# First layer of a two-block stack: the order of LayerNorm work on VectorE, and how the last output tile is cut

## Chip, cores, metric

The kernel runs on one core of one Trainium2 chip. The metric is the device time of one execution in microseconds (us). Before the change the median of four executions is 1633.42 us (1633.33 to 1634.01).

A core has five engines with a queue of instructions each: TensorE (PE: matrix products; its weight loads are listed apart as PEld), VectorE (DVE), ScalarE (ACT), GpSimd (POOL) and SyncE (SP, which here issues all DMA transfers). An engine takes its instructions in order. An instruction that has to wait holds up all that stand behind it on the same engine.

## What is computed

The input is x, 2048 tokens by 1024 features in bf16. Two blocks alternate, A, B, A, B, each with a LayerNorm ahead of it and a residual sum behind it:

```python
def _A_ref(x, wqkv, wo):           # linear attention, 32 heads of 32
    ...
    q, k, v = qkv[0], qkv[1], qkv[2]
    phi = lambda t: jnp.where(t > 0, t + 1, jnp.exp(t)) + 1e-6
    pq, pk = phi(q), phi(k)
    kv = jnp.einsum("bhsd,bhse->bhde", pk, v)
    z = jnp.einsum("bhsd->bhd", pk)
    num = jnp.einsum("bhqd,bhde->bhqe", pq, kv)
    den = jnp.einsum("bhqd,bhd->bhq", pq, z)[..., None] + 1e-6
    o = num / den
    return (...o...) @ wo

def _B_ref(x, w_gate, w_up, w_down):
    g = jnp.einsum("bsd,df->bsf", x, w_gate)
    u = jnp.einsum("bsd,df->bsf", x, w_up)
    h = g * u
    return jnp.einsum("bsf,fd->bsd", h, w_down)

x = x + _A_ref(_layernorm(x, axis=-1), A_wqkv, A_wo)
x = x + _B_ref(_layernorm(x, axis=-1), B_w_gate, B_w_up, B_w_down)
...
```

The last two lines run twice; the inner width of block B is 3584.

## The kernel before

The tokens are cut into 16 tiles of 128 (`NT`), four tiles to a group (`TPG`). `X` holds all of them on the core, and is the residual stream. The instructions of each engine stand in the order in which the program text emits them; no scheduler moves them. So "ahead of" in the text is "ahead of" in the queue.

**A unit of the first layer.** `k_unit(t)` and `q_unit(t)` are 16 matmuls each: 8 slices of the feature axis, times two halves of 512 output columns (`both`, line 204). The stationary operand is `xT`, the normalised tile t turned so that features lie on the partitions. `phi` (lines 209 to 214) follows: ScalarE makes `e` = exp and the positive part from the PSUM tile, then VectorE makes min(e, 1) + eps (line 213) and adds the two (line 214). The PSUM tiles that units use (`mm`) rotate through three buffers, and ScalarE is their last reader. `e` rotates through three buffers too, freed by line 214.

**What a unit needs.** `norm(t)` makes `xT` for tiles 4 to 15, in three steps. `ln_stats(t)`: VectorE takes two half-row statistics (line 183) and joins them to mean and variance (line 185), then GpSimd adds epsilon (line 187) and takes the power -1/2 (line 189), which gives `rstd`. `ln_apply(t)`: VectorE writes the normalised tile into `XN` (line 194) and needs `rstd` for it. `turn` (line 198): SP issues a transposing DMA from `XN` into `xT`. Tiles 0 to 3 are handled apart at the very start: they are only centred, turned by TensorE, and their `rstd` goes in as the scale inside `phi`. So their `XN` must be normalised later by a separate `ln_apply`, and only the products behind the q and k units (`g_unit`) read it.

**The order around the change.** After tiles 0 to 3 have had their k units, VectorE gets four `ln_apply` for tiles 0 to 3. Then `weave(main, fill)` alternates one entry of each list. `main` is q0 to q3, k4 to k7, q4 to q7, k8 to k15. `fill` is `norm(4)` to `norm(15)`, then `zs(...)` entries. Each `zs` adds the k rows of one or more tiles onto the running sum `zacc` (line 258). After the weave come `zs(13, 14, 15)` and `z_split` (lines 262, 263), which splits `zacc` into two bf16 parts. TensorE goes on with `g_unit(0)`, `g_unit(1)` and then `z_sum`, whose matmuls read these two parts.

**The end.** The last tile of the last layer is computed in pieces by `d_end` (line 487 for the matmuls), each piece 28 matmuls over the inner width, followed by a residual sum on VectorE (line 468) and a store to the output (line 470). All other tiles go through `d_unit` in one piece of 1024 columns.

Of the kernel before, what the change touches and what calls it, by code (L numbers as in the profile page):

```python
# [15 lines left out]
def weave(main, fill, first=0, step=1):  # L16

    out, fill = [], list(fill)
    for i, u in enumerate(main):
        out.append(u)  # L20
        if fill and i >= first and (i - first) % step == 0:
            out.append(fill.pop(0))
    return out + fill
# [3 lines left out]
def kernel(  # L27
# [15 lines left out]
    NT = S // P  # L43
# [4 lines left out]
    TPG = G // P  # L48
# [27 lines left out]
    def rows(ap, n):  # L76
        return ap.rearrange("p (t n) -> p t n", n=n)
# [85 lines left out]
    def mm_tile():  # L163
        return psum.tile([P, 2, NB], F32, tag="mm", bufs=3, name="ps")
# [7 lines left out]
    def idle(n):  # L172
        for _ in range(n):
            nc.tensor.matmul(out=zps[:, 0, :], lhsT=xT[3][:, 0, 0:P], rhs=xT[3][:, 0, :], start=True, stop=True)
# [5 lines left out]
    def ln_stats(t):  # L180
        st = small.tile([P, 2, 6], F32, tag="st", name="st")
        for c in range(2):
            nc.vector.bn_stats(out=st[:, c, :], in_=X[:, t, c * NB:(c + 1) * NB])  # L183
        mv = small.tile([P, 2], F32, tag="mv", bufs=NT, name="mv")
        nc.vector.bn_aggr(out=mv[:], in_=st[:])  # L185
        ve = small.tile([P, 1], F32, tag="ve", name="ve")
        nc.gpsimd.tensor_scalar(out=ve[:], in0=mv[:, 1:2], scalar1=1e-5, scalar2=None, op0=ALU.add)  # L187
        rstd = small.tile([P, 1], F32, tag="rstd", bufs=NT, name="rstd")
        nc.gpsimd.tensor_tensor(out=rstd[:], in0=ve[:], in1=mhalf[:], op=ALU.pow)  # L189
        stat[t] = (mv, rstd)  # L190

    def ln_apply(t, dst):
        mv, rstd = stat[t]
        nc.vector.tensor_scalar(out=dst, in0=X[:, t, :], scalar1=mv[:, 0:1], scalar2=rstd[:],  # L194
                                op0=ALU.subtract, op1=ALU.mult)

    def turn(src, slot, tl):
        nc.sync.dma_start_transpose(out=xT[slot][:, :, tl * P:(tl + 1) * P], in_=src)
# [22 lines left out]
    def layer_A(li):  # L221
        first = li == 0
        XN, PK = (rows(R1[:], D), rows(R2[:], D)) if first else (rows(R2[:], D), rows(R1[:], D))
# [6 lines left out]
        def k_part(t, a, b):  # L230
            if a == 0:
                open_ps[t] = mm_tile()
            ps = open_ps[t]
            tl = t % TPG
            for k in range(a, b):
                both(ps, xT[t // TPG][:, k, tl * P:(tl + 1) * P], wkv[:, k, :], k == 0, k == KD - 1)
            if b == KD:
                phi(ps, PK[:, t, :], scale_of(t))

        def k_unit(t):  # L240
            return lambda: k_part(t, 0, KD)
# [4 lines left out]
        def q_unit(t, later=None):  # L246
            def run():
                ps = mm_tile()
                tl = t % TPG
                for k in range(KD):  # L250
                    both(ps, xT[t // TPG][:, k, tl * P:(tl + 1) * P], wq[:, k, :], k == 0, k == KD - 1)
                phi(ps, q_slot(t), scale_of(t), later)
            return run

        def z_unit(t):
            def run():
                in0 = PK[:, 0, :] if t == 1 else zacc
                nc.vector.tensor_tensor(out=zacc, in0=in0, in1=PK[:, t, :], op=ALU.add)
            return run
# [77 lines left out]
        def norm(t, stats=True):  # L337
            def run():
                if stats:
                    ln_stats(t)  # L340
                ln_apply(t, XN[:, t, :])
                turn(XN[:, t, :], t // TPG, t % TPG)
            return run

        def zs(*ts):
            return lambda: [z_unit(t)() for t in ts]

        if first:
            def centre(t, mean):
                nc.vector.tensor_scalar(out=XN[:, t, :], in0=X[:, t, :], scalar1=mean, scalar2=None, op0=ALU.subtract)  # L350

            pts = {}

            def turn_pe(t):
                if t == 1:
                    pts[t] = psum.tile([P, KD, P], BF16, tag="mm", bufs=3, name="pt1")
                else:
                    pts[t] = psum.tile([P, KD, P], BF16, tag="kv", bufs=1, name="pt")
                for k in range(KD):
                    nc.tensor.transpose(out=pts[t][:, k, :], in_=XN[:, t, k * P:(k + 1) * P], identity=ident[:])  # L360
                nc.scalar.copy(out=xT[0][:, 0:4, t * P:(t + 1) * P], in_=pts[t][:, 0:4, :])

            def turn_rest(t):
                nc.vector.tensor_copy(out=xT[0][:, 4:8, t * P:(t + 1) * P], in_=pts[t][:, 4:8, :])

            mean1 = small.tile([P, 1], F32, tag="mean1", bufs=1, name="mean1")
            junk = small.tile([P, D], BF16, tag="eb", bufs=3, name="junk")

            idle(9)
            ln_stats(0)  # L370
            centre(0, stat[0][0][:, 0:1])
            nc.scalar.activation(out=junk[:], in_=X[:, 1, :], func=ACT.Copy, scale=1.0 / D, accum_out=mean1[:])  # L372
            turn_pe(0)
            idle(1)
            centre(1, mean1[:])
            turn_pe(1)
            ln_stats(2)
            centre(2, stat[2][0][:, 0:1])
            turn_rest(0)
            turn_rest(1)  # L380
            for t in range(2):
                k_part(t, 0, 2)
            for t in range(2):
                k_part(t, 2, 3)
            turn_pe(2)
            for t in range(2):
                k_part(t, 3, 4)
            ln_stats(3)
            centre(3, stat[3][0][:, 0:1])
            turn_rest(2)  # L390
            ln_stats(1)
            k_part(2, 0, 4)
            turn_pe(3)
            turn_rest(3)
            for t in range(3):
                k_part(t, 4, 8)
            k_part(3, 0, 8)
            for t in range(TPG):
                ln_apply(t, XN[:, t, :])
            main = [q_unit(t) for t in range(4)] + [k_unit(t) for t in range(4, 8)] + [q_unit(t) for t in range(4, 8)]  # L400
            main += [k_unit(t) for t in range(8, 16)]
            fill = [norm(t) for t in range(4, 16)]
            fill += [zs(1, 2), zs(3, 4), zs(5, 6), zs(7), zs(8), zs(9), zs(10, 11), zs(12)]
            do(weave(main, fill))
            do([zs(13, 14, 15), z_split])
        else:
            main = [k_unit(t) for t in range(4)] + [q_unit(t) for t in range(4)]
            main += [k_unit(t) for t in range(4, 8)] + [q_unit(t) for t in range(4, 8)]
            main += [k_unit(t) for t in range(8, 16)]
            fill = [norm(t, False) for t in range(12, 16)]  # L410
            fill += [zs(1), zs(2), zs(3)] + [lambda: None] * 2
            fill += [zs(4), zs(5), zs(6), zs(7)] + [lambda: None] * 3 + [zs(8), zs(9), zs(10), zs(11)]
            do(weave(main, fill))
            do([zs(12, 13, 14, 15), z_split])
# [22 lines left out]
        fill = [lambda t=t: ln_stats(t) for t in range(4)] + [b_norm(t) for t in range(4)]  # L437
# [5 lines left out]
    def b_norm(t, stats=False):  # L443
        def run():
            if stats:
                ln_stats(t)
            xn = tail[t % 2]
            ln_apply(t, xn)
            turn(xn, t // TPG % 2, t % TPG)
        return run  # L450
# [16 lines left out]
    def add_store(t, a, b, ps, last):  # L467
        nc.vector.tensor_tensor(out=X[:, t, a:b], in0=X[:, t, a:b], in1=ps, op=ALU.add)  # L468
        if last:
            nc.sync.dma_start(out=o_view[:, t, a:b], in_=X[:, t, a:b])  # L470
# [10 lines left out]
    def d_end(t):  # L481
        def run():
            tl = t % TPG
            for a, b in ((0, 512), (512, 768), (768, 1024)):
                ps = mm_tile()
                for f in range(KF):
                    nc.tensor.matmul(out=ps[:, 0, 0:b - a], lhsT=hT[:, f, tl * P:(tl + 1) * P], rhs=wd[f][:, a:b],  # L487
                                     start=(f == 0), stop=(f == KF - 1))
                add_store(t, a, b, ps[:, 0, 0:b - a], True)
        return run  # L490

    def do(units):
        for u in units:
            u()
# [37 lines left out]
    def prefetch(i, last):  # L532
# [6 lines left out]
        return run  # L539

    layer_A(0)
    layer_B(1)
    layer_A(2)
    layer_B(3)

# [29 lines left out]
```

## Time and profile before

| | us |
|---|---|
| median of four executions | 1633.42 |
| the profiled execution, its own time | 1634.01 |
| its span, first to last instruction | 1632.1 |
| TensorE busy in the span | 1618.0 |
| VectorE busy | 608.3 |
| ScalarE busy | 287.1 |
| GpSimd busy | 53.7 |

The granted TensorE clock is 1.00 over the whole span. A profile line of a group reads: start, duration, engine, source line, operation, what is written from what, shapes, count, and in brackets how long the engine had been idle just before and what ended that. A matmul's recorded duration is longer than the distance to the next one, since matmuls are pipelined: a stretch of equal matmuls is read from start to start. Times of the span count from its first instruction.

The VectorE work in the stretch that the change touches, by mean duration of one instruction (ns):

| line | what | mean ns |
|---|---|---|
| 183 | statistics of half a tile (two per tile) | 682 |
| 185 | joining them | 209 |
| 194 | normalising a tile | 543 |
| 213 | phi, first step | 424 |
| 214 | phi, sum | 693 |
| 258 | adding a tile to `zacc` | 1222 |
| 468 | residual sum, 1024 / 512 / 256 columns | 1222 / 689 / 421 |

### The profile page before, as it was taken

How to read it: one execution, taken by the hardware profiler on the slowest of the kernel's cores; microseconds unless marked ns; L12 is line 12 of the kernel's file. 1: busy time of each engine (PE TensorE's matmuls, PEld its weight loads, DVE VectorE, ACT ScalarE, POOL GpSimd, SP SyncE). 2: the span in 40 equal slices, each digit the busy share in tenths (PEclk: the TensorE clock that was granted, in tenths of full speed). 3: DMA queues.
4: the chain of work that ended last, by engine and by line, in shares of the span. 5: the costliest groups of instructions: out<-in, count | busy, mean ns of one | idle time of the engine just before them, and what ended most of it. 6: DMA issues, size and time to landing. Idle time of an engine off the chain costs nothing.

```text
span 1632.1 us, 17617 instructions
## 1 busy us (share of the span) xinstructions
PE 1618.0 (99%) x7510; PEld 743.0 (46%) x7662; DVE 608.3 (37%) x889; ACT 287.1 (18%) x386; POOL 53.7 (3%) x141
## 2 busy tenths in 40 slices
PE   9999999999999999999999999999999999999999
PEld 4444444444444444444444444444444444444444
DVE  6799853211311221243245698432123113211111
ACT  5523201100110110011045222011011101101110
POOL 1100000000000000010000000000000000000000
DMA  6324755521550453142420258565226405521400
GB/s 219 65 65 110 233 161 159 163 66 52 143 192 1 120 166 102 48 150 66 87 63 1 78 104 232 155 174 161 65 88 176 143 20 174 161 65 65 155 0 27
DMA packets 234686, 182.56 MB, mean 112 GB/s; under 512 B 100080, under 2 KB 215408, under 8 KB 234608
## 3 DMA queue, kind: packets, MB, share of 16 engines
q1 hardware_dynamic: 234608, 181.43, 38.3%
q8 instruction: 60, 0.98, 0.3%
q14 instruction: 18, 0.15, 0.0%
HBM read 153.09 MB, written 4.19 MB: 96 GB/s over the span
## 4 chain that ended last, share of the span: by engine, by line
PE 98%; DVE 1%; issue 1%; DMA 0%; POOL 0%; ACT 0%; SPq 0%; DVEq 0%
PE ps L204 49%; PE ps L460 47%; PE ps L487 1%; PE kv L301 0%; DVE st L183 0%; PE pm L204 0%; DMA X<-in_A_x_dram 0%; DMA xT<-R 0%; DVE PQ L214 0%; POOL rstd L189 0%; DVE R L194 0%; PE pt L360 0%; ACT junk L372 0%; ACT PQ L210 0%; DVE e L213 0%
## 5 line engine op out<-in xcount | busy, mean ns | idle before, releaser
L460 PE MATMUL ps<-xT,R 128*128 128x512 bf16 x2382 | 525.9, 379 | 2.7
L460 PEld LDWEIGHTS <-R 128*128 128x128 bf16 x2432 | 238.0, 98 | 286.9
L464 DVE TENSOR_TENSOR R<-gs,ps 128x512 bf16<-128x512 f32 x224 | 154.0, 688 | 533.3 <-ACT gs L463 533.3
L204 PEld LDWEIGHTS <-R 128*128 128x128 bf16 x2248 | 219.8, 98 | 264.5 <-issue 0.3
L463 ACT COPY gs<-ps 128x512 f32<-128x512 f32 x224 | 131.3, 586 | 1039.2 <-PE ps L460 1013.4
L460 PE MATMUL ps<-xT,W 128*128 128x512 bf16 x1130 | 250.1, 379 | 1.1
L204 PEld LDWEIGHTS <-xT 128*128 128x128 bf16 x1536 | 149.3, 98 | 179.2 <-DMA xT<-R 1.8
L204 PE MATMUL ps<-W,xT 128*128 128x512 bf16 x1001 | 225.2, 379 | 2.0 <-DMA xT<-R 0.8
L460 PEld LDWEIGHTS <-W 128*128 128x128 bf16 x1152 | 112.7, 98 | 135.9
L204 PE MATMUL ps<-W,R 128*128 128x512 bf16 x730 | 169.3, 379 | 0.7
L468 DVE TENSOR_TENSOR X<-X,ps 128x1024 bf16<-128x1024 bf16 (+2 forms) x34 | 39.4, 1159 | 335.9 <-PE ps L204 304.4
L204 PE MATMUL ps<-R,R 128*128 128x512 bf16 x501 | 112.4, 379 | 0.7
L204 PE MATMUL ps<-PQ,R 128*128 128x512 bf16 x487 | 111.3, 379 | 0.5
L204 PE MATMUL ps<-R,xT 128*128 128x512 bf16 x502 | 110.3, 379 | 0.5
L209 ACT ACTIVATE e<-ps 128x1024 bf16<-128x1024 f32 x56 | 57.4, 1024 | 146.5 <-PE ps L204 91.0
L183 DVE BATCH_NORM_STATS2 st<-X 128x6 f32<-128x512 bf16 x128 | 81.9, 682 | 2.2 <-DMA X<-in_A_x_dram 2.0
L187 POOL TENSOR_SCALAR ve<-mv 128x1 f32<-128x1 f32 x64 | 15.4, 241 | 1337.9 <-DVE mv L185 1337.9
L204 PE MATMUL ps<-GL,R 128*128 128x512 bf16 x242 | 58.1, 379 | 0.4
L204 PE MATMUL ps<-xT,R 128*128 128x512 bf16 x242 | 57.9, 379 | 0.3
L334 DVE TENSOR_TENSOR X<-X,ps 128x1024 bf16<-128x1024 bf16 x32 | 38.8, 1213 | 28.0 <-PE ps L204 27.2
L194 DVE TENSOR_SCALAR R<-X,mv,rstd 128x1024 bf16<-128x1024 bf16 x64 | 33.7, 543 | 36.0 <-POOL rstd L189 36.0
L213 DVE TENSOR_SCALAR e<-e 128x1024 bf16<-128x1024 bf16 x64 | 27.1, 424 | 43.0 <-ACT e L209 43.0
(62 smaller groups left out, 461.0 us busy)
## 6 DMA issues: line engine op xcount, KB each, us to landing
R<-in_B_w_gate_dram SPq DMA_DIRECT2D x38, 1024.0 KB, 5.5
R<-in_B_w_up_dram SPq DMA_DIRECT2D x38, 1024.0 KB, 7.5
W<-in_B_w_gate_dram SPq DMA_DIRECT2D x18, 1024.0 KB, 5.4
W<-in_B_w_up_dram SPq DMA_DIRECT2D x18, 1024.0 KB, 7.4
W<-in_A_wqkv_dram SPq DMA_DIRECT2D x10, 1024.0 KB, 6.5
W<-in_B_w_down_dram SPq DMA_DIRECT2D x6, 1024.0 KB, 11.4
PQ<-in_B_w_down_dram SPq DMA_DIRECT2D x4, 1024.0 KB, 8.1
X<-in_A_x_dram SPq DMA_DIRECT2D x15, 256.0 KB, 6.5
```

Source lines behind the costliest of these rows:

```text
L183: nc.vector.bn_stats(out=st[:, c, :], in_=X[:, t, c * NB:(c + 1) * NB])
L187: nc.gpsimd.tensor_scalar(out=ve[:], in0=mv[:, 1:2], scalar1=1e-5, scalar2=None, op0=ALU.add)
L194: nc.vector.tensor_scalar(out=dst, in0=X[:, t, :], scalar1=mv[:, 0:1], scalar2=rstd[:], op0=ALU.subtract, op1=ALU.mult)
L204: nc.tensor.matmul(out=ps[:, n, :], lhsT=lhsT, rhs=rhs[:, n * NB:(n + 1) * NB], start=start, stop=stop)
L209: nc.scalar.activation(out=e[:], in_=flat(ps), func=ACT.Exp, **sc)
L213: nc.vector.tensor_scalar(out=e[:], in0=e[:], scalar1=1.0, scalar2=EPS, op0=ALU.min, op1=ALU.add)
L334: nc.vector.tensor_tensor(out=X[:, t, :], in0=X[:, t, :], in1=flat(ps), op=ALU.add)
L460: nc.tensor.matmul(out=ps[:, n, :], lhsT=w[:, k, j * P:(j + 1) * P], rhs=xT[g % 2][:, k, :], start=(k == 0), stop=(k == KD - 1))
L463: nc.scalar.copy(out=gs[:], in_=ps[:, 0, :])
L464: nc.vector.tensor_tensor(out=hT[:, f, :], in0=gs[:], in1=ps[:, 1, :], op=ALU.mult)
L468: nc.vector.tensor_tensor(out=X[:, t, a:b], in0=X[:, t, a:b], in1=ps, op=ALU.add)
L487: nc.tensor.matmul(out=ps[:, 0, 0:b - a], lhsT=hT[:, f, tl * P:(tl + 1) * P], rhs=wd[f][:, a:b], start=(f == 0), stop=(f == KF - 1))
```

## The change

In the first layer the statistics of tile 4 are taken ahead of the weave. Each of the twelve normalising entries then normalises its own tile, turns it, and takes the statistics of the tile after it. The four `ln_apply` for tiles 0 to 3 go from ahead of the weave into four entries behind the normalising ones, each with one addition to `zacc`; the later additions are grouped two to an entry. In `d_end` the second and third piece of the last tile are 384 and 128 columns wide in place of 256 and 256.

```diff
-            for t in range(TPG):
-                ln_apply(t, XN[:, t, :])
+            ln_stats(4)
+
+            def norm_step(t):
+                def run():
+                    norm(t, False)()
+                    if t + 1 < NT:
+                        ln_stats(t + 1)
+                return run
+
+            def xn_and_z(t, *ts):
+                return lambda: [ln_apply(t, XN[:, t, :])] + [z_unit(u)() for u in ts]
+
...
-            fill = [norm(t) for t in range(4, 16)]
-            fill += [zs(1, 2), zs(3, 4), zs(5, 6), zs(7), zs(8), zs(9), zs(10, 11), zs(12)]
+            fill = [norm_step(t) for t in range(4, 16)]
+            fill += [xn_and_z(0, 1), xn_and_z(1, 2), xn_and_z(2, 3), xn_and_z(3, 4), zs(5, 6), zs(7, 8), zs(9, 10),
+                     zs(11, 12)]
             do(weave(main, fill))
             do([zs(13, 14, 15), z_split])
...
-            for a, b in ((0, 512), (512, 768), (768, 1024)):
+            for a, b in ((0, 512), (512, 896), (896, 1024)):
```

The number of matmuls, activations, GpSimd instructions and DMA issues stays as it is, and so does their order on each of those engines. On VectorE the set of instructions is the same too; only their order changes.

## The prediction

> **What bounds the kernel now.** I began with the page: busy time by engine, then the shares of the chain that ended last.
>
> ```profile
> PE 1618.0 (99%) x7510; PEld 743.0 (46%) x7662; DVE 608.3 (37%) x889; ACT 287.1 (18%) x386; POOL 53.7 (3%) x141
> PE 98%; DVE 1%; issue 1%; DMA 0%; POOL 0%; ACT 0%; SPq 0%; DVEq 0%
> ```
>
> TensorE is busy 1618.0 of 1632.1 us, and the chain is TensorE's for 98%. No matmul is removed, so only the 14.1 us in which TensorE stands still can be won. The waits of TensorE over the whole span say where it waits for another engine: 1.2 and 0.7 us in the opening, which the change leaves alone, and this one:
>
> ```profile
> PE ps L204 <- DMA xT<-R: 0.8, 1, 0.8
> ```
>
> The chain in order of time places it: a transposing DMA of 3.39 us ends, and the unit behind it (k7) starts at 47.51.
>
> ```profile
> 44.07 3.39 DMA xT<-R
> 47.46 0.05 issue
> 47.51 6.86 PE ps L204 x31
> ```
>
> Its full price is read from ScalarE in the timeline: one exp per unit, started by the unit's last matmul. These are k4, k5, k6, k7, q4:
>
> ```profile
> 39.68 1.02 ACT L209 ACTIVATE e<-ps 128x1024 bf16<-128x1024 f32 x1 [1.33 <-PE ps L204]
> ...
> 43.13 1.02 ACT L209 ACTIVATE e<-ps 128x1024 bf16<-128x1024 f32 x1 [1.52 <-PE ps L204]
> ...
> 46.72 1.02 ACT L209 ACTIVATE e<-ps 128x1024 bf16<-128x1024 f32 x1 [1.65 <-PE ps L204]
> ...
> 51.17 1.02 ACT L209 ACTIVATE e<-ps 128x1024 bf16<-128x1024 f32 x1 [2.52 <-PE ps L204]
> ...
> 54.62 1.02 ACT L209 ACTIVATE e<-ps 128x1024 bf16<-128x1024 f32 x1 [1.52 <-remote]
> ```
>
> The distances are 3.45, 3.59, 4.45, 3.45. An undisturbed unit takes 3.45, so k6 lost 0.14 and k7 1.00: 1.14 us. (The 0.83 of idle time in the waits counts from the modelled end of a matmul, 379 ns after its start, where the stream goes on after 216.) Why the tile is late, VectorE shows in the same timeline, one round of its work:
>
> ```profile
> 42.29 0.21 DVE L185 BATCH_NORM_AGGREGATE mv<-st 128x2 f32<-128x12 f32 x1
> 42.59 0.22 POOL L187 TENSOR_SCALAR ve<-mv 128x1 f32<-128x1 f32 x1 [3.24 <-DVE mv L185]
> ...
> 43.50 0.55 DVE L194 TENSOR_SCALAR R<-X,mv,rstd 128x1024 bf16<-128x1024 bf16 x1 [1.00 <-POOL rstd L189]
> 43.96 0.42 DVE L213 TENSOR_SCALAR e<-e 128x1024 bf16<-128x1024 bf16 x1
> ...
> 46.41 0.21 DVE L185 BATCH_NORM_AGGREGATE mv<-st 128x2 f32<-128x12 f32 x1
> ```
>
> From one joining of statistics to the next it is 4.12 us, of which 1.00 is VectorE standing for GpSimd's rstd. TensorE takes a unit every 3.45. VectorE falls back 0.67 a unit, and by tile 7 it is too late.
>
> **Part 1, the statistics ahead.** Removed: the 1.00 of waiting, twelve times (12.0 us in VectorE's waits). A round is then 4.12 - 1.00 = 3.12, below 3.45, so VectorE follows ScalarE and waits there instead. What is queued behind that new wait is the normalisation: it now stands behind the unit's phi, which needs ScalarE's second activation. I place it from the rows of before. Those activations end at 27.99 (q0), 31.44 (q1), 34.89 (q2) and 38.35 (q3); line 214 starts 0.03 later and lets the next instruction start 0.61 after that. So the normalisations of tiles 4 to 7 start at 28.6, 32.1, 35.5 and 39.0 (before: 31.15, 35.26, 39.38, 43.50). With 0.55 for themselves and 3.4 for the transfer (the four landed after 3.0 to 3.4), the tiles are there at 32.6, 36.0, 39.5 and 42.9. TensorE wants them at 36.2, 39.7, 43.1 and 46.6: some 3.6 us to spare each time. The stall goes: -1.14.
>
> GpSimd's pair lies under phi: joined at 26.7, rstd at 27.65, wanted at 28.6. Should GpSimd be slower by more than that 0.95, the rest comes out of the 3.6. Statistics of tile 4 start at 25.17, right behind the phi of k3; the input transfers' traffic falls to almost nothing at 25, and tile 4 leads the twelve late input tiles, so I cost its wait at nothing (3.6 covers it too). SP's twelve transposes keep their order and pass no other issue: SP had issued the input loads by 22.1. Cadence of the transfers becomes 3.45 where one takes 3.0 to 3.4, so they still don't overlap.
>
> **Part 2, the four normalisations and the sums moved.** Four times 0.48 us (start to start) leave the front and come back in the rounds of k8 to k11, which are then 0.53 + 0.61 + 0.48 + 1.26 = 2.88, below 3.45. Rounds with two sums (k12 to k15) take 3.66, falling back 0.2 each, 0.6 by the third. What is late next would be the split of zacc, wanted by TensorE after the second g unit:
>
> ```profile
> 104.71 1.23 DVE L263 TENSOR_TENSOR W<-GL,W 128x1024 bf16<-128x1024 f32 x1
> ...
> 106.42 1.03 PE L204 MATMUL ps<-W,ones 128*128 128x512 bf16 x4
> ```
>
> Before, it ended at 105.94, a mere 0.48 ahead of its reader. After: the last activation of k15 ends at 94.55 - 1.14 = 93.4; line 214 takes 0.6, five sums 6.3, the split 1.95, plus the 0.6 of backlog: 102.9, against 106.42 - 1.14 = 105.28. Spare: 2.4. Cost: nothing, covered by the two g units of TensorE. If VectorE had not become quicker, the cover would end at 105.94 and 0.66 of the 1.14 would be given back.
>
> **Part 3, the last pieces.** Here the end of the span is the chain itself:
>
> ```profile
> 1622.63 1.04 PE L487 MATMUL ps<-PQ,R 128*128 128x256 bf16 x8
> ...
> 1625.69 1.04 PE L487 MATMUL ps<-PQ,R 128*128 128x256 bf16 x8
> ...
> 1628.94 0.42 DVE L468 TENSOR_TENSOR X<-X,ps 128x256 bf16<-128x256 bf16 x1 [2.64 <-PE ps L487]
> ```
>
> 28 matmuls of 256 columns take 3.06 us, 109.3 ns each; with 512 columns 216. That is 0.417 ns a column and 2.6 ns, so 384 columns cost 162.7 ns. For 128 columns with a fresh weight load each, the nearest row is the kv products:
>
> ```profile
> 107.29 0.61 PE L301 MATMUL kv<-GL,W 128*128 128x128 bf16 x8
> ```
>
> (0.61 - 0.219 of one) / 7 = 56 ns. Both pieces: 28 x (162.7 + 56) = 6.12, as before (2 x 3.06): nothing. That row is a run of 8, not 28. The bound above: a weight load's 98 ns each if loads could not overlap, 28 x 42 = +1.18. Below nothing isn't open, since 128 columns by the slope are 56. I take 56, because the load hides behind the product in the row itself. Page "TensorE: Matmul & The Clock Gate" of the Trainium skill, section "Back-to-back issue gap", speaks against the change: it gives about 81 ns for a sustained stream of load and 128-column matmul. By that rule the piece would cost 28 x 25 = 0.70 more, and the whole gain would shrink to 0.6.
>
> The last sum falls from 421 to about 287 ns (an estimate: 689 - 421 = 268 for 256 columns, half of that off): -0.13; bounds 0 and -0.21 (half of 421). The 384-column sum, about 0.55, and its store lie under the 1.57 us of the last piece. The last store is 32 KB for 64: stores of 128 KB and 64 KB landed in 1.7 and 1.6, so -0.05. Bounds: -0.1, and +0.3 if rows of 256 bytes take twice the 0.3 us in which the 64 KB moved. Section "Specifications" of "DMA: Bandwidth & Descriptors" in the skill says that under 512 B the engine reads, modifies and writes; every store here had rows of 512 B or more, so no row answers.
>
> **Sum.** -1.14 - 0.13 - 0.05 = -1.3 us. The profiled execution took 1634.01 (span 1632.1, with 1.9 around it) and was the slowest of the four; it would be 1632.7. From the median: 1633.42 - 1.3 = **1632.1**. This is 0.08%, under the 0.2% (3.3 us) that a measurement of this kernel can tell from no change.
>
> **Rivals.**
> - The stall stays, because the normalisation behind phi waits for ScalarE as it did for GpSimd: only part 3 remains, 1633.42 - 0.18 = 1633.2. For it: the new wait is real. Against: 3.6 us to spare. Ten in a hundred.
> - The stall goes but the narrow piece gives it back: +1.18 and +0.3 against -1.14 - 0.13: 1633.6. For it: no 28 narrow matmuls in a row exist in the trace, nor a 256-byte store. Against: eight run at 56. With half-way cases, 12 in a hundred.
> - Slower: the last piece runs at the pace of the longest weight load in the trace, 152 ns (in the opening transposes). 28 x (152 - 56) = +2.7, less 1.3: 1634.8. It decides from 56 + 1.3/28 = 103 ns a matmul up. Against: that row belongs to the opening; at the end the loads are 97 to 98. Four in a hundred.
>
> The forecast has 74. **Range**: the best ends give -1.14 - 0.21 - 0.1 = -1.45, 1632.0; the runs scatter from -0.1 to +0.6 around their median, and I allow 0.5 below. Above, it reaches the first rival and most of the second: 1631.4 to 1633.5. Faster by over 0.2% would need 3.3 us, more than all stalls named; 6 in a hundred for what I don't see. Slower by over 0.2% needs the narrow piece above 220 ns or the split 7.0 us later than worked out (2.4 to spare, 1.3 to give back, 3.3): 4. Within: 90.
>
> **What would show it.** Part 1 right: no wait of TensorE for xT, the exps of k4 to k7 all 3.45 apart, GpSimd gone from VectorE's waits. Part 2: the split done 2 us or more ahead of z_sum's first matmul. Part 3: last piece about 1.6 us from first to last matmul, last sum near 0.29. I am wrong if a wait on VectorE or for xT shows up after 47 us, or if the stretch from the first 384-column matmul to the last sum is over 6.4 us.

## The result and the profile after

| | before | after |
|---|---|---|
| median of the executions, us | 1633.43 (61) | 1631.92 (41) |
| lowest | 1633.00 | 1631.43 |
| profiled execution, own time | 1634.01 | 1631.71 |
| its span | 1632.1 | 1629.8 |

The ratio of the times is 0.999, with a 95% interval of 0.9986 to 0.9995. The median moved by 1.51 us, 0.09%: less than 0.2%, and in the direction and near the size that was forecast (1632.1). The interval leaves 1 out, so over this many executions even less than 0.2% is told from no change. The trace has the two profiled spans to the hundredth, 1632.06 and 1629.82; they differ by 2.24 us, 0.7 more than the medians, and where the rest comes from is shown in the last section.

First the waits of TensorE over the whole span in the kernel after, columns as before: who waited for whom, us in total, times, longest.

```profile
PE ps L174 <- DVE xT L169: 1.2, 1, 1.2
```

That is the whole list. The wait for `xT` is gone. (The 0.7 us in the opening that stood there before is gone as well. It isn't the change's: in the other profiles, of old and new order, the same wait is between 0.3 and 1.2 us in all; see the last section.) The timeline of the kernel after has the exps of k4, k5, k6, k7 and q4 here:

```profile
39.01 1.02 ACT L209 ACTIVATE e<-ps 128x1024 bf16<-128x1024 f32 x1 [1.33 <-PE ps L204]
...
42.47 1.02 ACT L209 ACTIVATE e<-ps 128x1024 bf16<-128x1024 f32 x1 [1.51 <-PE ps L204]
...
45.92 1.02 ACT L209 ACTIVATE e<-ps 128x1024 bf16<-128x1024 f32 x1 [1.52 <-PE ps L204]
...
49.37 1.02 ACT L209 ACTIVATE e<-ps 128x1024 bf16<-128x1024 f32 x1 [1.52 <-PE ps L204]
...
52.83 1.02 ACT L209 ACTIVATE e<-ps 128x1024 bf16<-128x1024 f32 x1 [1.51 <-remote]
```

The distances are 3.45 or 3.46 all the way. From k4 to q4 it is 13.82 us where it was 14.94, so 1.12 us are won. One round of VectorE in the same timeline:

```profile
36.64 0.21 DVE L185 BATCH_NORM_AGGREGATE mv<-st 128x2 f32<-128x12 f32 x1
36.77 0.37 DVE L213 TENSOR_SCALAR e<-e 128x1024 bf16<-128x1024 bf16 x1
36.94 0.28 POOL L187 TENSOR_SCALAR ve<-mv 128x1 f32<-128x1 f32 x1 [2.52 <-DVE mv L185]
37.30 0.57 POOL L189 TENSOR_TENSOR rstd<-ve,mhalf 128x1 f32<-128x1 f32 x1
37.71 0.69 DVE L214 TENSOR_TENSOR PQ<-PQ,e 128x1024 bf16<-128x1024 bf16 x1 [0.57 <-ACT PQ L210]
38.32 0.54 DVE L194 TENSOR_SCALAR R<-X,mv,rstd 128x1024 bf16<-128x1024 bf16 x1
...
40.09 0.21 DVE L185 BATCH_NORM_AGGREGATE mv<-st 128x2 f32<-128x12 f32 x1
```

A round is 3.45 us, TensorE's pace. GpSimd's pair runs under the phi, and the bracket at line 214 shows the new wait: 0.57 us for ScalarE. The normalisation at line 194 waits for nobody, and GpSimd is gone from the list of VectorE's waits. The end of the span:

```profile
1625.18 0.61 PE L498 MATMUL ps<-PQ,R 128*128 128x128 bf16 x8
1625.38 0.56 DVE L479 TENSOR_TENSOR X<-X,ps 128x384 bf16<-128x384 bf16 x1 [3.86 <-PE ps L498]
...
1626.52 0.39 PE L498 MATMUL ps<-xT,R 128*128 128x128 bf16 x4
1626.95 0.29 DVE L479 TENSOR_TENSOR X<-X,ps 128x128 bf16<-128x128 bf16 x1 [1.01 <-PE ps L498]
```

28 narrow matmuls start from 1625.18 on, the first 24 of them within 1.34 us: 56 ns each. The last sum is 0.29 us, and from its start to the end of the span it is 2.87 us, where it was 3.11.

### The profile page after: what moved, and what is told of

Same layout as the page of the kernel before. It is cut to its first block, busy times and chain, and to the rows that moved or that the text cites. A ratio compares the mean times of both kernels' runs of the same rounds, so it can differ in the third digit from the quotient of the medians.

```text
span 1629.8 us, 17605 instructions
## 1 busy us (share of the span) xinstructions
PE 1617.6 (99%) x7510; PEld 742.2 (46%) x7662; DVE 607.8 (37%) x889; ACT 287.3 (18%) x386; POOL 55.2 (3%) x141
## 4 chain that ended last, share of the span: by engine, by line
PE 99%; issue 1%; DVE 0%
PE ps L204 50%; PE ps L471 47%; PE ps L498 1%; PE kv L301 0%; PE ps L174 0%; PE pm L204 0%; PE pt L360 0%; DVE X L479 0%; DVE xT L169 0%
## 5 line engine op out<-in xcount | busy, mean ns | idle before, releaser
L479 DVE TENSOR_TENSOR X<-X,ps 128x1024 bf16<-128x1024 bf16 (+3 forms) x34 | 39.4, 1159 | 335.7 <-PE ps L204 304.4
L276 DVE TENSOR_TENSOR tmp<-PQ,GL 128x1024 f32<-128x1024 bf16 x32 | 39.0, 1220 | 11.1 <-ACT GL L269 10.9
```

The costliest lines, as they stand in the source:

```text
L276: nc.vector.tensor_tensor(out=tmp[:], in0=q, in1=zacc, op=ALU.mult)
```

## The experiments

Each kernel ran eleven times beside the kernel before on the same chip; the kernel before had a median of 1633.45 us beside the first four and of 1633.60 beside the others. The scatter of eleven runs leaves a mean uncertain by 0.1 to 0.2 us (one standard error), and the 95% intervals that stand with the ratios are wider, some 1.4 us to either side. So effects of a few tenths are read from the profiles, where a distance between two instructions holds to some hundredths as long as no wait for a DMA lies between them.

**The last pieces alone.**

```diff
-            for a, b in ((0, 512), (512, 768), (768, 1024)):
+            for a, b in ((0, 512), (512, 896), (896, 1024)):
```

> The kernel before with only the last pieces cut anew (384 and 128 columns). Theory: the narrow matmuls run at 56 ns, the last sum falls from 421 to about 290 ns and the last store from issue to the end of the span gets 0.17 us shorter, so -0.3 us against before (-0.02%) and the opening and the first layer as before: k7 is still 1.0 us late. Rival (narrow matmuls at 81 ns): the last piece takes 0.7 us more, so +0.4 us.

Measured: 1633.35 us, -0.10, ratio 0.9999 (0.9990 to 1.0008). By the median alone the gain isn't told from nothing. The profile tells it: from the first 384-column matmul (1622.03) to the last sum (1628.35) 6.32 us, the same as the 6.31 of two pieces of 256, and from there to the end of the span 2.88, against 2.87 in the kernel after and 3.11 before. The rival, +0.7 us for narrow matmuls, has fallen.

**The new order alone.** The pieces stay 256 and 256, the rest is as in the change.

> The changed kernel with the old pieces (256 and 256). Theory: the wait for xT (1.13 us) is gone, and also 0.2 us that the first g unit lost in the kernel before because it reads the k rows of tile 15, which VectorE finished at 99.03 when TensorE wanted them at about 98.9: together -1.3 us (-0.08%). From the exp of k15 to the first g copy 6.91 us (before 7.11). Rival (the 0.2 us and the 0.66 us in the opening belong to the new order): -1.8 to -2.0 us, and the opening 0.66 us shorter than before in every profile of the new order.

Measured: 1632.16 us, -1.29, ratio 0.9992 (0.9983 to 1.0000). From k4 to q4 13.82 us, from the exp of k15 to the first g copy 6.91. So the order is worth about 1.3 us and the pieces the rest. The rival has fallen too: the opening is not shorter in every profile of the new order (last section).

The 0.2 us named there were not in the forecast. In ScalarE's timeline of the kernel before, the exp of k15 and the copies behind the two g units are:

```profile
92.61 1.02 ACT L209 ACTIVATE e<-ps 128x1024 bf16<-128x1024 f32 x1 [1.51 <-PE ps L204]
...
99.72 1.01 ACT L291 CAST GL<-ps 128x1024 bf16<-128x1024 f32 x1 [5.17 <-PE ps L204]
106.62 1.01 ACT L291 CAST GL<-ps 128x1024 bf16<-128x1024 f32 x1 [5.89 <-PE ps L204]
```

The second g unit takes 6.90 us, the first 7.11. The timeline of VectorE and the weight loads in the kernel before shows what it stumbled over:

```profile
98.34 0.69 DVE L214 TENSOR_TENSOR R<-R,e 128x1024 bf16<-128x1024 bf16 x1
...
99.09 0.96 PEld L204 LDWEIGHTS <-R 128*128 128x128 bf16 x5 [0.32 <-issue]
```

Line 214 is the phi of k15, done at 99.03. The first g unit multiplies all 16 tiles, with the k rows as the moving operand, and takes tile 15 last. Its matmuls start 0.216 us apart in the trace; the one that first reads tile 15's k rows starts at 99.09, 0.42 after the one ahead of it, so 0.20 late. The weight load behind it sits idle for 0.32 us. TensorE's list of waits doesn't have this wait, because the list counts idle time from a matmul's modelled end, 379 ns after its start: of the 0.20 only 0.04 is left. The next experiment but two tests that reading.

The two losses, at `xT` and here, are not independent. From the exp of k3 to the first g copy it is 77.31 us in the kernel before (22.41 to 99.72) and 77.31 in the kernel with only the pieces changed (21.81 to 99.12), although the stall at `xT` is 0.05 shorter there. The phi of k15 is done 76.63 us after the exp of k3 in both. It is VectorE's backlog that sets the time; a shorter stall at `xT` only makes the first g unit wait longer. In every profile in which the statistics are taken ahead, the same stretch is 75.97 us: 1.34 less.

**The statistics ahead, and nothing moved.**

```diff
             for t in range(TPG):
                 ln_apply(t, XN[:, t, :])
+            ln_stats(4)
...
-            fill = [norm(t) for t in range(4, 16)]
+            fill = [norm_step(t) for t in range(4, 16)]
```

> Only the statistics one tile ahead; the four normalisations of tiles 0 to 3 stay in front and the sums stay grouped as before; old pieces. Theory: VectorE's round falls to 3.12 us, so the 1.9 us in front is made up in time, the wait for xT goes and the k rows of tile 15 are in time too: -1.3 us, the same as the whole new order. Rival (the move of the four normalisations is what makes tile 7 come in time): k6 or k7 still late, -0.5 us or less.

Measured: 1631.90 us, -1.55, ratio 0.9991 (0.9982 to 0.9999). No wait for `xT`, 6.90 us to the first g copy, and the split of `zacc` even earlier than in the kernel after: done at 100.59, wanted at 104.57. That is the whole gain of the new order; the rival has fallen. But the round of 3.12 us did not come. VectorE still waits for GpSimd, 0.46 us a round (5.5 us in all, where it was 12.0), and a round is 3.53 us, slightly more than TensorE's 3.45:

```profile
DVE R L194 <- POOL rstd L189: 5.5, 12, 0.5
```

```profile
28.39 0.69 DVE L214 TENSOR_TENSOR PQ<-PQ,e 128x1024 bf16<-128x1024 bf16 x1
28.45 1.06 POOL L189 TENSOR_TENSOR rstd<-ve,mhalf 128x1 f32<-128x1 f32 x1
...
29.55 0.55 DVE L194 TENSOR_SCALAR R<-X,mv,rstd 128x1024 bf16<-128x1024 bf16 x1 [0.46 <-POOL rstd L189]
```

The line is of VectorE's waits, the three below it of the timeline. GpSimd's line 189 starts just behind VectorE's line 214 here and takes 1.06 us. In the kernel after VectorE waits for ScalarE ahead of line 214, line 189 starts ahead of it and takes 0.57. So VectorE was fast enough here with some 2.4 us to spare for tiles 4 to 7 (landing of the tile to the start of its unit), where the kernel after has 3.8 to 4.0, and not for the reason that was expected.

**The move alone.** The four normalisations and the sums stand where the change puts them, but each tile's statistics stay in the entry that normalises it.

> Only the four normalisations moved and the sums regrouped; statistics stay in the same entry as their normalisation, so VectorE still stands for GpSimd 1.0 us a round; old pieces. Theory: nothing is won in front (the phi of q0 waits for ScalarE until 28.0 anyway), k7 is still 1.0 us late; at the end VectorE has 1.9 us more to do, so the k rows of tile 15 come 0.66 us later and the split of zacc ends near 107.9 where z_sum wants it at 106.4: TensorE stands some 1.4 us more, so +1.4 us (+0.09%) against before. Rival (the move wins the time in front): -0.5 to -1.1 us.

Measured: 1634.47 us, +1.02, ratio 1.0007 (0.9998 to 1.0015). The waits of TensorE in this kernel:

```profile
PE ps L204 <- DMA xT<-R: 1.0, 2, 0.6
...
PE ps L204 <- DVE R L214: 0.4, 1, 0.4
PE ps L204 <- DVE W L263: 0.2, 1, 0.2
```

Besides those of the opening there are three waits: for `xT` (k6 and k7 lose 0.81 and 0.55, 1.36 where it was 1.13 before), for the phi of k15, and for the split. In exps and copies: +0.23 at k6 and k7, +0.36 to the first g copy (7.47 for 7.11), +0.35 from the second g copy to that of z_sum (1.26 for 0.91). The sum is 0.94, beside 1.02 measured. How the first two split is an accident of this execution: the normalisations of tiles 4 to 7 start 8.7, 12.9, 17.0 and 21.1 us after the exp of k3 as they did before, but the transposing DMA of tile 6 took 3.72 us in this execution, where it took 3.05. Their sum is not, since the phi of k15 is done 77.21 us after the exp of k3, 0.58 later than before. The expectation had 1.4 because it took the split as wanted by the first matmul of z_sum. Two of the four matmuls read only the first half, from line 262, and started at once; the wait fell on the other two:

```profile
106.20 0.59 PE L204 MATMUL ps<-W,ones 128*128 128x512 bf16 x2
107.03 0.59 PE L204 MATMUL ps<-W,ones 128*128 128x512 bf16 x2 [0.23 <-DVE W L263]
```

**The kernel before, with one sum behind the phi of k15.**

```diff
-            fill += [zs(1, 2), zs(3, 4), zs(5, 6), zs(7), zs(8), zs(9), zs(10, 11), zs(12)]
+            fill += [zs(1, 2), zs(3, 4), zs(5, 6), zs(7), zs(8), zs(9), zs(10), zs(11, 12)]
```

> The kernel before with one addition to zacc (tile 11) moved behind the phi of k15. Theory: the phi of k15 is done 1.26 us earlier, so the first g unit no longer waits for the k rows of tile 15: from the exp of k15 to the first g copy 6.91 us (before 7.11), -0.2 us; the wait for xT stays at 1.13 us. Rival (the 0.2 us were a stumble of TensorE's own): 7.11 us as before, no change.

Measured: 1633.09 us, -0.51, ratio 0.9998 (0.9990 to 1.0007). ScalarE's timeline of this kernel:

```profile
92.22 1.02 ACT L209 ACTIVATE e<-ps 128x1024 bf16<-128x1024 f32 x1 [1.52 <-DVE e L213]
...
99.13 1.01 ACT L291 CAST GL<-ps 128x1024 bf16<-128x1024 f32 x1 [4.97 <-PE ps L204]
```

6.91 us: the first g unit had waited for VectorE. The wait for `xT` is there as before (0.7 in the list of waits). The median moved by more than the 0.2 us that was expected. The profile shows why it may: from the exp of k3 to the first g copy it is 76.90 us (22.23 to 99.13), 0.41 less than before. The transposing DMA of tile 7 took 3.20 us in this execution and 3.39 in that of the kernel before, so the stall came out 0.2 shorter (14.74 us from k4 to q4), and with the phi of k15 done earlier nothing takes that back.

**Statistics ahead with the new pieces.**

> Statistics ahead, the four normalisations and the grouping of the sums left as before, pieces of 512, 384 and 128. Theory: the move of the four normalisations is worth nothing, so this is as fast as the changed kernel: -1.6 us against before, within 0.2 us of the changed kernel. Rival (the move matters by freeing the front): 0.3 us or more slower than the changed kernel.

Measured: 1631.86 us, -1.74, ratio 0.9990 (0.9981 to 0.9999), within 0.1 us of the kernel after by the medians, and 0.2 below it when each is set against the kernel before that ran beside it. VectorE's wait for GpSimd is 5.5 us again. The move takes that wait away, but adds nothing to the time.

**Other widths of the last piece**, on the kernel after: 64 columns (512, 448, 64), and 512 (512, 512).

> The changed kernel with pieces of 512, 448 and 64 columns. Theory (56 ns is the pace of a weight load with its matmul, and 128 columns happen to hide under it): the 28 matmuls of 64 columns don't go below about 56 ns, 27 ns over the column slope, so +0.75 us for them, -0.07 for the last sum, -0.05 for the store: +0.6 us against the changed kernel, -0.9 us against before. Rival (the slope of 0.417 ns a column goes on, 29 ns a matmul): -0.1 us against the changed kernel, -1.6 us against before.

> The changed kernel with two last pieces of 512 columns, so that a 512-column sum and a 128 KB store end it. Theory (the end costs what the last sum and the last store cost): the last sum 0.69 us for 0.29, the store longer by 0.2 to 0.3: +0.6 to +0.7 us against the changed kernel, -0.9 us against before. Rival (the medians show no effect of the last piece, as in the run of the pieces alone, -0.10 us): within 0.2 us of the changed kernel, -1.4 us against before.

Measured: 1631.93 us with 64 columns (-1.67, ratio 0.9990, 0.9981 to 0.9999) and 1632.73 with 512 (-0.87, ratio 0.9994, 0.9985 to 1.0004). The timeline of the kernel with 64 columns:

```profile
1626.47 0.40 PE L498 MATMUL ps<-PQ,R 128*128 128x64 bf16 x8
...
1627.17 0.28 PE L498 MATMUL ps<-xT,R 128*128 128x64 bf16 x4
1627.49 0.22 DVE L479 TENSOR_TENSOR X<-X,ps 128x64 bf16<-128x64 bf16 x1 [0.20 <-PE ps L498]
```

24 matmuls take 0.70 us, 29 ns each with a weight load for each: the column slope goes on, and my theory of a pace of 56 ns has fallen. Nothing is won all the same. The end, over all profiles:

| columns of the last piece | last sum, us | its start to the end of the span, us | store, issue to landing, us |
|---|---|---|---|
| 512 | 0.69 | 3.42 | 1.7 |
| 256 (five profiles) | 0.42 | 3.09 to 3.11 | 1.6 |
| 128 (three profiles) | 0.29 | 2.87 to 2.88 | 1.5 |
| 64 | 0.22 | 2.84 | 1.5 |

(The third column is taken with spans to the hundredth, from the traces.) With 512 columns the end is 0.55 us longer than with 128, near the 0.6 to 0.7 expected, and the rival (no effect of the last piece) has fallen. From 256 to 128 it is 0.23 us, from 128 to 64 only 0.04: the last sum gets 0.07 shorter, but its store lands 0.03 later after its issue, and that issue took SP 0.38 us in place of 0.33, 0.42 us behind the start of the one before. What lengthens it isn't shown. None of the versions beats the kernel after by more than the scatter.

## Why the prediction was right, step by step

**Part 1** held in mechanism and size. It had the normalisations of tiles 4 to 7 start at 28.6, 32.1, 35.5 and 39.0. In the profile after they start at 27.96, 31.42, 34.87 and 38.32, each 0.6 to 0.7 earlier, since the whole first layer starts 0.66 earlier in that execution (exp of q0 at 25.20 for 25.86). Predicted -1.14, measured -1.12 between k4 and q4. The size holds for that execution of the kernel before: in three profiles of the old order the stall was 0.9 to 1.1 us, as the transposing DMA of tile 7 took 3.2 to 3.4. GpSimd's pair got longer but stayed under the phi: `rstd` is there 0.75 us ahead of the first normalisation (0.95 was worked out) and 0.27 to 0.45 ahead of the later ones. It stays there only because the front was freed as well; with the statistics ahead alone 0.46 us of the wait was left in each round. The first rival, a wait for ScalarE in the place of the one for GpSimd, was half right: the wait exists, 0.57 us a round, but the tiles still land 3.8 to 4.0 us ahead of their units (3.6 was worked out).

**Part 2** named the right cover, and one reader too few. The split was worked out with 2.4 us to spare; it is done at 101.87 where z_sum starts at 104.43, 2.56. (The half that line 263 writes is first read by z_sum's third matmul, so the true spare time is larger, before and after.) But "what is late next would be the split" was not all: the first g unit wants the phi of k15 earlier still, and in the kernel before it already waited 0.2 us for it. The quicker VectorE wins that too. The step that failed is the reading of the list of waits as complete, when a wait shorter than the modelled overlap of two matmuls (379 less 216 ns) leaves almost nothing in it. (With the move alone the same wait cost 0.56 us, and the list has 0.4.) The same step makes "0.66 of the 1.14 would be given back" too small: with VectorE no quicker, the phi of k15 would still have been done 76.63 us after the exp of k3, and the first g unit would have given back the whole 1.14. That is worked out from the two profiles of the old order above; no run takes away the stall alone.

**Part 3** was right in sign, and small: -0.18 forecast, -0.24 in the profiles. The last sum got 0.13 shorter as forecast, and the store landed 0.10 sooner after its issue (1.49 for 1.59), in place of 0.05. Both prices against the piece were refuted by rows: 56 ns a matmul in a run of 28, where the Trainium skill's page "TensorE: Matmul & The Clock Gate", section "Back-to-back issue gap", gives about 81, and no slower store of 256-byte rows (landing 1.5 us for 1.6).

**The sum** by the profiles is -1.12 - 0.20 - 0.24 = -1.6 us, beside -1.51 between the medians and -1.3 forecast. The forecast is short by the 0.20 that it didn't see and by a part of the store.

How much later VectorE could get before `xT` is late again was not tried.

## What to carry to other kernels

Where an engine does a short chain through another one (statistics here, a power there, then the use here), issue the chain for the next item between this item's steps. Here the round trip then cost nothing where the first engine had idle time of its own, and 0.46 in place of 1.00 us where it had none. The gain downstream is bounded by what the bottleneck engine really waited, here 1.3 of 12.0 us of removed waiting. Before costing a later consumer of an engine's backlog, list every reader in the order in which the bottleneck engine reaches it, and measure equal units against each other, since a list of waits can leave out a short one. Two waits behind one late engine don't add up: winning the first alone would have lengthened the second here. Work moved off the front of an engine's queue gained nothing here, where the next instruction there waited for another engine anyway.

## What was not expected

The opening scatters from one execution to the next. ScalarE's first pass over the second input tile, which waits for that tile to land, starts at 4.25 to 5.43 us in the ten profiles, and the exp of k3 at 21.61 to 22.52, in old and new order alike. The profile of before was one of the late ones and that of after an early one (22.41 and 21.75); this makes 0.66 of the 2.24 us between their spans. Nothing shows that it belongs to the change: both kernels have the same instructions up to there, and the latest exp of k3 (22.52) is of the new order.

GpSimd's line 187 takes 223 ns (median of the twelve in the weave) in the kernel before and 365 ns in the kernel after, where it runs beside VectorE's line 213. It costs nothing there. Line 189 takes 0.57 us in both kernels (the first of the twelve 0.78 in the kernel after); where it took 1.06, with the statistics ahead alone, VectorE waited for it.

A matmul with its own weight load can follow the last one in 29 ns at 64 columns, although the profile gives each load 98 ns.
